# A chunked mLSTM cell and gelu block on one core: two weight sums made one chunk earlier, and one row copy set between two gelu halves

## The chip, the cores and the metric

The kernel runs on one core of one Trainium2 chip. The metric is the device time of one execution in microseconds (us), as the median over several executions. The engines are named as the profile names them: PE is TensorE (matmuls) and PEld its weight loads, DVE is VectorE, ACT is ScalarE, POOL is GpSimd, SP is SyncE, whose queue issues most of the DMAs. All of them run side by side and wait for each other by semaphores.

## What is computed

```python
def _attn_ref(q, k, v, i_gate, f_gate, o_gate):      # B, H, S, D = 4, 8, 768, 40
    for t in range(S):
        m_new = np.maximum(f_gate[:, :, t] + m, i_gate[:, :, t])
        f_stab = np.exp(f_gate[:, :, t] + m - m_new)
        i_stab = np.exp(i_gate[:, :, t] - m_new)
        C = f_stab * C + i_stab * outer(v_t, k_t)
        n = f_stab * n + i_stab * k_t
        y[:, :, t] = sigmoid(o_t) * (C @ q_t) / np.maximum(np.abs(n . q_t), 1.0)

x = y.transpose(0, 2, 1, 3).reshape(3072, 320)
h = x @ w_in                                          # w_in 320 x 2048
g = h * (1.0 / (1.0 + np.exp(-1.702 * h)))
return g @ w_out                                      # w_out 2048 x 320
```

All data are float32. The weights come as 64-bit words of which the kernel makes float32 on the core.

## The kernel before

**Chunks.** The 768 steps are cut in six chunks `w` = 0 to 5 of 128 steps (for all four batches, so 512 tokens a chunk). For each chunk the kernel has two parts that PE runs one after the other: the first product (`x @ w_in`, 16 blocks of 128 hidden columns taken as eight pairs `j`) with the gelu, and the second product (`g @ w_out`). The attention part of the next chunk (scores, values, the carried state, gates) is cut in pieces and put between the blocks of the second product: `attention(w + 1)` gives a table of pieces by block number, and the loop at L986 runs block `i` and then the pieces of that number. The schedule is manual: the order in which the program issues instructions is the order on each engine, and an instruction waits for the data and buffers it needs.

**First chunk and later chunks.** In chunk 0 the products are plain (`up`, L614, and `down`, L785, the latter 16 calls of four matmul groups, blocks 0 to 15). From chunk 1 on they are Strassen-like fast products (`up_fast`, L707, and `down_fast`, L831) of seven block products in place of eight. They need sums of the blocks of the weights. `weight_sums(n)` (L801) makes the four sums of the second weights, each one POOL subtraction of 128 x 1280 elements: n = 0 gives `t1 = w01 - w00`, n = 1 gives `t2 = w11 - t1`, n = 2 overwrites `w01` with `w11 - w01`, n = 3 gives `t4 = w10 - t2`. `w00` to `w11` are quarters of `w_out_sb`, and `t1`, `t2`, `t4` lie in `t_sb`, whose room holds keys of chunk 1 (`k_1`, read by PE for the transposes and in `carry`, L594) and a piece of raw weights before. The first product of the sums is the third block of `down_fast(1, 0)`.

**A pair in `up_fast`.** For each pair `j` PE makes products into four PSUM banks: `p1`, `p56` and two row banks `row0`, `row1`. `ps_m` is a pool of four banks taken in turn, `ps_a` one of two double banks. At j = 0 and j = 4 (`k == 0`) the row banks are fresh ones of `ps_m`, and PE then adds the products of the last 64 input columns for four pairs (`row_product`, L694, matmuls at L701), into two pairs of `ps_a` banks and, for pair j + 1, into the two banks that `p1` and `p56` had. So the `p1` of pair 5 takes the bank that `row0` of pair 4 had. For each pair ACT copies `p1` (L761), DVE makes the sums (L762, L763, L774, L775), ACT copies `row0` into `g` (`copy_row`, L739, for j < 6), and POOL adds the DVE sums to it (L781). The gelu of pair j - 1 (`gelu_fast`, L688: half 1, then half 0, both L690) is issued in pair j; half 1 needs only DVE's L775 of pair j - 1, half 0 needs POOL's L781 of pair j - 1. In pairs with `k == 2` `copy_row` is called early, before L761; in the others it is called after both gelu halves.

**POOL in chunk 1.** After pair 0, `gates(2)` runs on DVE (L288 to L326) and `wait_for(ends[2])` (L592, a copy of one column into `mark`) makes POOL wait for it. Then `weight_sums(j)` follows each of the pairs 0 to 3, and `hidden_difference` (L812, POOL) follows the pairs 2 to 5.

**Around the first chunk's scores.** `scores(1, 0)` and `scores(1, 1)` come behind block 6: PE's L459, then one DVE multiplication each (L462, into `wt[1, 0]` and `wt[1, 1]`). Behind block 8 come `values(1, 0)` and the transfers `seam_out`/`seam_in` of its half, behind block 9 `values(1, 1)` and the transfers of the other half, behind blocks 12 and 14 the two `seam_turn` (L572), which fill the `xT` that the next first product reads; behind blocks 11 and 13 the `input_sums` (L668 to L671). `values` ends in `outputs` (L464): DVE's L517 and L518, three small ones (L469, L470, L471), L473, and two L478, which write the `y` that `seam_out` sends. `token_sums` (L679 to L684) then makes the sums of `xT` for the fast product; L682 makes `x4`, the right-hand side of product 4. All of this is one queue of DVE.

Of the kernel before, what the change touches and what calls it, by code (L numbers as in the profile page):

```python
# [26 lines left out]
def kernel(  # L27
# [141 lines left out]
    wt = {(0, b): gp.tile([L, NP, 2, L], FP, tag="g", name="wt") for b in range(B)}  # L169
# [63 lines left out]
    def convert(n):  # L233
        convert_begin(n)
        convert_end(n)
# [101 lines left out]
    def banks(name):  # L337
        return ps_a.tile([128, 2, 512], FP, tag="a", name=name)
# [251 lines left out]
    def wait_for(x):  # L590

        G.tensor_copy(out=mark[0:x.shape[0]], in_=x[:, 0:1])  # L592
# [92 lines left out]
        temps[w] = {1: b11, 2: b21, 3: b22, 4: x4, 5: x1, 6: x2, 7: b12}  # L685
        second[w] = r[1][:, half_w:W]

    def gelu_fast(w, j):  # L688
        for i in (1, 0):
            A.activation(out=gs[w, j][:, i, :], in_=gs[w, j][:, i, :], func=AF.Gelu_apprx_sigmoid)  # L690

    row_banks = {}

    def row_product(w, j, start):  # L694

        n = 2 if w == NW - 2 or (w == NW - 3 and j < 2) else 1
        for h in range(n):
            t = slice(h * W // n, (h + 1) * W // n)
            for i, row in enumerate(row_banks[w, j]):
                r = slice(i * 64, i * 64 + 64)  # L700
                T.matmul(row[:, t], w_in_x[r, j, :], xT[w][r, 2].rearrange("p b t -> p (b t)")[:, t],  # L701
                         start=(start and h == 0), stop=(not start and h == n - 1))

    def bank(name="p_h"):
        return ps_m.tile([128, W], FP, tag="m", name=name)

    def up_fast(w, j):  # L707

        x = temps[w]
        k = j % 4
        left, right = slice(0, half_w), slice(half_w, W)
        f = lambda c, i: w_in_sb[:, c, (2 * j + i) * 128:(2 * j + i + 1) * 128]

        def product(n, out, start, stop):
            a = {1: lambda: f(0, 0), 2: lambda: f(1, 0), 3: lambda: s_in[:, 2, j], 4: lambda: f(1, 1),  # L720
                 5: lambda: s_in[:, 0, j], 6: lambda: s_in[:, 1, j], 7: lambda: f(0, 1)}[n]()
            T.matmul(out, a, x[n], start=start, stop=stop)  # L722

        def row_0():
            product(2, row0[:, left], k == 0, False)
            product(3, row0[:, right], False, k > 0)

        def row_1():
            product(4, row1[:, left], k == 0, False)
            product(7, row1[:, right], False, k > 0)  # L730

        y = work.tile([L, 2, DM + 64], FP, tag="y", name="parts").rearrange("p a b -> p (a b)")
        u2 = second[w]
        g = gs[w, j] = gp.tile([128, 2, W], FP, tag="g", name="g")
        apart = j < NF // 2 - 2

        def copy_row():
            if apart:
                A.copy(out=g[:, 0, :], in_=row0)  # L739

        if k == 2:
            row0, row1 = row_banks[w, j]
            row_1()
            row_0()
        p1, p56 = bank(), bank()
        if k == 0:
            row0, row1 = row_banks[w, j] = bank(), bank()
        elif k != 2:
            row0, row1 = row_banks[w, j]
        product(1, p1[:, left], True, True)  # L750
        if k == 0:
            row_0()
        product(5, p56[:, left], True, True)
        product(6, p56[:, right], True, True)
        if k != 2:
            row_1()
        if k % 2:
            row_0()
        if k == 2:
            copy_row()  # L760
        A.copy(out=y[:, left], in_=p1[:, left])  # L761
        V.tensor_tensor(out=u2, in0=p56[:, right], in1=y[:, left], op=OP.add)  # L762
        V.tensor_tensor(out=y[:, 2 * half_w:3 * half_w], in0=p56[:, left], in1=u2, op=OP.add)  # L763
        if k == 0:
            row_product(w, j, False)
            for n in (2, 3):
                both = banks("p_h")
                row_banks[w, j + n] = both[:, 0, :], both[:, 1, :]
                row_product(w, j + n, True)
            row_banks[w, j + 1] = bank(), bank()  # L770
            row_product(w, j + 1, True)
        if j:
            gelu_fast(w, j - 1)
        V.tensor_tensor(out=y[:, half_w:2 * half_w], in0=row1[:, right], in1=u2, op=OP.add)  # L774
        V.tensor_tensor(out=g[:, 1, :], in0=row1, in1=y[:, half_w:3 * half_w], op=OP.add)  # L775
        u = y.rearrange("p (a t) -> p a t", t=half_w)[:, 0:3:2]
        g0 = g[:, 0, :].rearrange("p (a t) -> p a t", a=2)
        if apart:
            if k != 2:
                copy_row()  # L780
            G.tensor_tensor(out=g0, in0=g0, in1=u, op=OP.add)  # L781
        else:
            V.tensor_tensor(out=g0, in0=row0.rearrange("p (a t) -> p a t", a=2), in1=u, op=OP.add)
# [17 lines left out]
    def weight_sums(n):  # L801
        out, a, b = ((t1, w01, w00), (t2, w11, t1), (w01, w11, w01), (t4, w10, t2))[n]
        G.tensor_tensor(out=out, in0=a, in1=b, op=OP.subtract)
# [60 lines left out]
    def run(calls):  # L864
        for f, *args in calls:
            f(*args)
# [62 lines left out]
    for w in range(NW):  # L929
        more = w + 1 < NW  # L930
        if w == 0:
            for j in range(NF // 2):
                if j % 2 == 0:
                    ahead, behind = converted[j // 2]
                    run([(convert, p) for p in ahead] + [(fetch, p) for p in fetched.get(j // 2, ())])
                    up(w, j, lambda: run([(columns_turn, 1) if p is None else (convert, p) for p in behind]))
                if j == 6:
                    load(1, "o")
                if j == 1:
                    wait_for(w_in_sb[:, 1, 512:1024])  # L940
                    scale(0, 1)
                    load(1, "v")
                if j < B and j % 2:
                    carry(0, j // 2)
                if j == 3:
                    masks()
                    gates(1)
                    columns_in(1)
                if j == 4:
                    spread(1)  # L950
                    load_squares(1, "q")
                if j >= B:
                    transposes(1, j - B)
        else:
            token_sums(w)
            for j in range(NF // 2):
                up_fast(w, j)
                if more and j == 0:
                    gates(w + 1)
                    load(w + 1, "o")  # L960
                    if w == 1:
                        wait_for(ends[w + 1])
                if w == 1 and j < 4:
                    weight_sums(j)
                if more and j == 2:
                    columns_in(w + 1)
                    spread(w + 1)
                    load(w + 1, "vk")
                if more and j:
                    for n in ((0, 2), (), (4,), (6, 1, 3), (5, 7), (), ())[j - 1]:  # L970
                        block_transposes(w + 1, n)
                if more and j == 7:
                    columns_turn(w + 1)
                if 2 <= j < 6:
                    hidden_difference(w, j - 2)
                if j >= 6:
                    hidden_sums(w, (j - 6,), G)
            gelu_fast(w, NF // 2 - 1)
            hidden_sums(w, (2, 3), V)
        side = attention(w + 1) if more else {}  # L980
        if w == 0:

            blocks = [(lambda b=b, n=n: down(w, b, n)) for n0 in (0, 2) for b in range(B) for n in (n0, n0 + 1)]
        else:
            blocks = down_fast(w, 0) + down_fast(w, 1)
        for i, block in enumerate(blocks):  # L986
            if w == 0 and i in (0, 4, 5):
                convert((17, 18, 19)[max(i - 3, 0)])
                if i == 0:
                    for n in (1, 3, 5, 7):  # L990
                        block_transposes(1, n)
            if w + 2 < NW and i == (6 if w == 0 else 0):
                load_gates(w + 2)
            if w + 2 < NW and i == 13:
                load_squares(w + 2, "kq" if w else "k")
            if w == 0 and i == 15:
                load_squares(w + 2, "q")
            block()
            run(side.get(i, []))
            if w == 0 and i in (11, 13):  # L1000
                input_sums(slice(0, 4) if i == 11 else slice(4, 8))

# [29 lines left out]
```

## Time and profile before

| what | value |
|---|---|
| median of 3 runs | 466.53 us (466.46 to 466.73) |
| span of the profiled execution | 464.1 us |
| PE busy | 456.6 us, 98% of the span, 5071 matmuls |
| PEld busy | 391.2 us, 84% |
| DVE busy | 349.2 us, 75% |
| ACT busy | 185.8 us, 40% |
| POOL busy | 162.8 us, 35%, 154 instructions |
| DMA | 52.87 MB, mean 114 GB/s |
| POOL's L803 (the weight sums) | 4 of 2.885 to 2.902 us |
| POOL's L781 | 30 of 1.256 to 1.286 us |
| ACT's L739 (`copy_row`) | 30 of 0.564 to 0.589 us |

The page gives the span of the profiled execution, not a device time of its own; the median of the runs is 2.4 us above this span. The span counts from the first to the last recorded instruction. Busy time is an average over stages: a matmul that is in flight counts as busy whether the clock is full or half. The second product of chunk 0 lies at 66 to 110 us of the span, the first product of chunk 1 at 109 to 145 us, its second product at 145 to 185 us; the first product of chunk 2 starts at 185 us.

### The profile page before, as it was taken

What the parts mean: (1) busy time and instruction counts of PE and PEld (TensorE: products, weight loads), DVE (VectorE), ACT (ScalarE), POOL (GpSimd) and SP (SyncE); (2) the same over time, 40 slices, a digit from 0 to 9 for tenths busy, and PEclk for the clock granted to TensorE, in tenths of its full rate; (3) what the DMA queues carried; (4) which work ended last, traced back from release to release, by engine and by line L of the source; (5) the groups of instructions that cost most, each with busy time, mean ns of one, the idle gap of its engine ahead of it and who ended that gap; (6) DMA issues with size and microseconds to landing.
All of it is one profiled execution on the core that took longest, in us unless ns stands there. A gap on an engine that the chain in (4) does not pass through costs nothing.

```text
span 464.1 us, 12384 instructions
## 1 busy us (share of the span) xinstructions
PE 456.6 (98%) x5071; PEld 391.2 (84%) x5071; DVE 349.2 (75%) x738; ACT 185.8 (40%) x433; POOL 162.8 (35%) x154
## 2 busy tenths in 40 slices
PE   8999999999989999999999999999999999999996
PEld 6867877776859999779999779999888999787996
DVE  6788998799958785888786888787788766553722
ACT  5686779000536700455800354900264910164200
POOL 5101508000797700266800167610157710146200
PEclk9999999999989999999999999999999999999999
DMA  8998999049976025969024978315999305000000
GB/s 169 187 295 187 253 239 204 4 106 198 149 157 78 3 59 123 200 113 189 9 58 107 194 119 162 53 33 125 175 140 156 63 18 140 29 1 1 1 28 30
DMA packets 135561, 52.87 MB, mean 114 GB/s; under 512 B 101984, under 2 KB 131632, under 8 KB 135504
## 3 DMA queue, kind: packets, MB, share of 16 engines
q1 hardware_dynamic: 127136, 50.27, 55.4%
q10 hardware_dynamic: 8048, 1.66, 1.8%
q8 instruction: 40, 0.66, 0.6%
q0 software_dynamic: 320, 0.15, 0.2%
q14 instruction: 17, 0.14, 0.1%
HBM read 44.52 MB, written 7.54 MB: 112 GB/s over the span
## 4 chain that ended last, share of the span: by engine, by line
PE 88%; SPq 4%; DMA 2%; issue 2%; DVE 2%; POOL 1%; ACT 1%; DVEq 0%; POOLq 0%; ACTq 0%
PE p_out L844 33%; PE p_h L722 24%; PE p_out L790 8%; PE p_h L701 7%; PE p_h L626 5%; SPq L122 3%; PE p_c L602 3%; PE p_o L503 2%; PE p_s L459 2%; PE p_i L511 2%; DMA s_in<-in_moe_w_in_dram 2%; PE p_h L635 2%; POOL g L781 1%; SPq L167 0%; PE p_t L386 0%
## 5 line engine op out<-in xcount | busy, mean ns | idle before, releaser
L781 POOL TENSOR_TENSOR g<-g,parts 128x512 f32<-128x512 f32 x30 | 38.2, 1272 | 196.5 <-ACT g L739 187.7
L761 ACT COPY parts<-p_h 128x256 f32<-128x256 f32 x40 | 14.9, 372 | 164.5 <-PE p_h L722 134.1
L844 PE MATMUL p_out<-w_out_sb,g 128*128 128x160 f32 x480 | 68.9, 300 | 0.0
L722 PE MATMUL p_h<-xT,w_in_sb 128*128 128x256 f32 x240 | 66.4, 385 | 2.0 <-ACT g L739 2.0
L844 PEld LDWEIGHTS p_out<-w_out_sb,g 128*128 128x128 f32 x480 | 66.4, 190 | 0.5
L690 ACT ACTIVATE g<-g 128x512 f32<-128x512 f32 x80 | 47.8, 629 | 30.1 <-DVE g L775 19.1
L722 PEld LDWEIGHTS p_h<-xT,w_in_sb 128*128 128x128 f32 x240 | 44.9, 191 | 14.2 <-issue 5.5
L849 DVE TENSOR_TENSOR o_sb<-o_sb,p_out 128x160 f32<-128x160 f32 x70 | 21.4, 317 | 44.2 <-PE p_out L844 43.6
L844 PE MATMUL p_out<-t_sb,s 128*128 128x160 f32 x320 | 47.1, 300 | 0.0
L844 PEld LDWEIGHTS p_out<-t_sb,s 128*128 128x128 f32 x320 | 44.4, 190 | 0.2
L722 PE MATMUL p_h<-t_x,s_in 128*128 128x256 f32 x160 | 42.0, 385 | 0.0
L435 ACT ACTIVATE wt<-wt,cols 128x64 f32<-128x64 f32 x160 | 38.8, 334 | 0.1
L701 PE MATMUL p_h<-xT,w_in_x 64*128 64x512 f32 (+1 forms) x200 | 37.1, 514 | 0.0
L790 PE MATMUL p_out<-w_out_sb,g 128*128 128x320 f32 x128 | 35.7, 436 | 0.0
L722 PEld LDWEIGHTS p_h<-t_x,s_in 128*128 128x128 f32 x160 | 31.0, 194 | 4.4
L762 DVE TENSOR_TENSOR t_x<-p_h,parts 128x256 f32<-128x256 f32 x40 | 16.9, 424 | 20.3 <-PE p_h L722 12.9
L790 PEld LDWEIGHTS p_out<-w_out_sb,g 128*128 128x128 f32 x128 | 23.9, 190 | 9.6
L701 PEld LDWEIGHTS p_h<-xT,w_in_x 64*128 64x128 f32 x200 | 18.5, 186 | 14.9 <-issue 13.9
L739 ACT COPY g<-p_h 128x512 f32<-128x512 f32 x30 | 17.5, 582 | 31.1 <-PE p_h L701 17.5
L626 PE MATMUL p_h<-xT,w_in_sb 128*128 128x256 f32 x128 | 29.6, 384 | 0.0
L775 DVE TENSOR_TENSOR g<-p_h,parts 128x512 f32<-128x512 f32 x40 | 27.6, 691 | 1.4
L626 PEld LDWEIGHTS p_h<-xT,w_in_sb 128*128 128x128 f32 x128 | 23.6, 190 | 5.3 <-issue 2.4
(205 smaller groups left out, 853.6 us busy)
## 6 DMA issues: line engine op xcount, KB each, us to landing
q_sq<-in_q_dram SPq DMA_DIRECT2D x20, 320.0 KB, 10.6
wt<-m_row SPq DMA_DIRECT2D x20, 256.0 KB, 5.4
k_sq<-in_k_dram SPq DMA_DIRECT2D x16, 320.0 KB, 6.0
out_dram<-o_sb SPq DMA_DIRECT2D x24, 160.0 KB, 1.9
eo<-in_o_gate_dram SPq DMA_DIRECT2D x5, 640.0 KB, 7.9
bits<-in_moe_w_in_dram SPq DMA_DIRECT2D x6, 512.0 KB, 11.3
q_sq<-x_row SPq DMA_DIRECT2D x10, 256.0 KB, 3.0
v_st<-in_v_dram SPq DMA_DIRECT2D x14, 160.0 KB, 5.7
```

The lines of the kernel that those rows point to most:

```text
L435: A.activation(out=x[:, h, :], in_=x[:, h, :], func=AF.Exp, scale=-1.0, bias=cols[w][:, c * PH + h:c * PH + h + 1])
L626: T.matmul(ph[j][i][:, t], w_in_sb[:, c, f * 128:(f + 1) * 128], x[:, c, t], start=(first and c == 0 and n == 0), stop=(not first and c == ...
L690: A.activation(out=gs[w, j][:, i, :], in_=gs[w, j][:, i, :], func=AF.Gelu_apprx_sigmoid)
L701: T.matmul(row[:, t], w_in_x[r, j, :], xT[w][r, 2].rearrange("p b t -> p (b t)")[:, t], start=(start and h == 0), stop=(not start and h == ...
L722: T.matmul(out, a, x[n], start=start, stop=stop)
L739: A.copy(out=g[:, 0, :], in_=row0)
L762: V.tensor_tensor(out=u2, in0=p56[:, right], in1=y[:, left], op=OP.add)
L775: V.tensor_tensor(out=g[:, 1, :], in0=row1, in1=y[:, half_w:3 * half_w], op=OP.add)
L781: G.tensor_tensor(out=g0, in0=g0, in1=u, op=OP.add)
L790: T.matmul(po, gs[w, f // 2][:, f % 2, b * L:(b + 1) * L], w_out_sb[:, f, :], start=(f == 0), stop=(f == NF - 1))
L844: T.matmul(po, a(f), b[:, f, :], start=(f == 0), stop=(f == NH - 1))
L849: V.tensor_tensor(out=dst, in0=x, in1=po, op=OP.add)
```

## The change

Two edits in the program, with one call site added and one loop bound altered.

1. The sums n = 0 and n = 1 are issued in chunk 0's second product, behind the pieces of block 6 (the scores of chunk 1), after a `wait_for` on one column of `wt[1, 0]`, which DVE's first L462 writes. In chunk 1's first product the sums n = 2 and n = 3 then follow the pairs 0 and 1; nothing follows the pairs 2 and 3.
2. In chunk 1's pair 4, `copy_row` is called between half 1 and half 0 of the gelu of pair 3, and no longer after it. No other pair and no other chunk is touched.

One POOL instruction (the added `wait_for`) is new; the number of all others is as before.

```diff
-    def gelu_fast(w, j):
+    def gelu_fast(w, j, between=None):
         for i in (1, 0):
+            if between and i == 0:
+                between()
             A.activation(out=gs[w, j][:, i, :], in_=gs[w, j][:, i, :], func=AF.Gelu_apprx_sigmoid)
...
+        early = w == 1 and j == 4
         if j:
-            gelu_fast(w, j - 1)
+            gelu_fast(w, j - 1, copy_row if early else None)
...
         if apart:
-            if k != 2:
+            if k != 2 and not early:
                 copy_row()
             G.tensor_tensor(out=g0, in0=g0, in1=u, op=OP.add)
...
-                if w == 1 and j < 4:
-                    weight_sums(j)
+                if w == 1 and j < 2:
+                    weight_sums(j + 2)
...
             block()
             run(side.get(i, []))
+            if w == 0 and i == 6:
+                wait_for(wt[1, 0][:, 0, 0, :])
+                weight_sums(0)
+                weight_sums(1)
```

## The prediction

> **What bounds the kernel now.** I read the chain that ended last first. From the start of chunk 0's products to the end it is PE almost throughout; the one place past 31 us where it leaves PE for long is chunk 1's first product, from 113.8 to 134.3 us, where it goes through DVE's gates, POOL's sums and ACT. Its end, with the same 42 matmuls in chunk 2 beside it (columns: start, length, what):
>
> ```profile
> 131.87 1.25 POOL g L781
> 133.11 0.02 issue
> 133.14 0.63 ACT g L690
> 133.77 0.48 ACT g L739
> 134.25 0.04 issue
> 134.29 11.02 PE p_h L722 x42
> ...
> 207.28 9.26 PE p_h L722 x42
> ```
>
> POOL's L781 (pair 3) lets ACT do half 0 of pair 3's gelu, behind which stands `copy_row` of pair 4, which frees the bank for pair 5. PE's last row product before it ends at 132.25 (L701, 128.55 + 3.70). And the 42 matmuls that follow take 11.02 us here, 9.26 in chunk 2. Second I asked for busy time and granted clock by stretches:
>
> ```profile
> 132.25:134.30 2.05, 0.01 (x2) 0.01 (x1) 1.86 (x3) 1.10 (x2) 2.05 (x2) 1.00 0.60 237
> 134.30:138.00 3.70, 3.70 (x9) 2.98 (x10) 0.81 (x2) 0.90 (x2) 3.70 (x3) 0.54 1.22 206
> ```
>
> The columns are length, PE, PEld, DVE, ACT, POOL busy, then granted clock. PE is idle for 2.04 us, POOL busy for all of it, and the clock is then 0.54 on average for 3.7 us. The loss of the place is 2.04 of idle time and 11.02 - 9.26 = 1.76 of slow matmuls, **3.80 us**. Chunks 2 to 5 have no such idle time on the chain.
>
> Third, POOL's order of time (start, length, instruction):
>
> ```profile
> 114.87 1.26 POOL L781 TENSOR_TENSOR g<-g,parts 128x512 f32<-128x512 f32 x1 [34.23 <-ACT g L739]
> ...
> 127.75 2.89 POOL L803 TENSOR_TENSOR w_out_sb<-w_out_sb 128x1280 f32<-128x1280 f32 x1
> 130.60 1.26 POOL L812 TENSOR_TENSOR g<-g 128x512 f32<-128x512 f32 x1
> 131.84 1.27 POOL L781 TENSOR_TENSOR g<-g,parts 128x512 f32<-128x512 f32 x1
> ```
>
> From 119.4 to 139.6 POOL works without a gap, four sums of 2.9 us among it, and pair 3's L781 stands behind three of them. Before it, POOL is idle from 80.6 to 114.9 us. Fourth, DVE's order of time, where the sums are to go:
>
> ```profile
> 70.27 1.45 DVE L257 TENSOR_SCALAR w_out_sb<-w_out_sb 128x512 uint32<-128x512 uint32 x1
> ...
> 87.61 2.35 DVE L462 TENSOR_TENSOR wt<-p_s,wt 128x1024 f32<-128x1024 f32 x2
> ...
> 93.87 0.17 DVE L469 TENSOR_SCALAR den<-u 128x16 f32<-128x16 f32 x1
> 94.08 0.18 DVE L470 TENSOR_TENSOR den<-u,den 128x16 f32<-128x16 f32 x1
> ...
> 100.94 0.49 DVE L794 COPY o_sb<-p_out 128x320 f32<-128x320 f32 x1 [0.44 <-PE p_out L790]
> ...
> 111.10 0.42 DVE L682 TENSOR_TENSOR t_x<-xT,t_x 128x256 f32<-128x256 f32 x1
> ```
>
> DVE has only 0.44 us of idle time between 92.1 and 112.9, the one shown before L794. Its `x4` (L682) is ready at 111.52 and PE's product 4 starts at 111.57: PE has no slack there.
>
> **Part 1, what is removed.** POOL's start stays: `mark` at 119.40, then a sum 119.54 to 122.41, L781 of pair 1 to 123.65, a sum to 126.52, L781 of pair 2 to 127.77, all as now, only that the sums are n = 2 and 3. Here the old third sum falls out. L812 for pair 0 runs 127.75 to 129.0. L781 of pair 3 needs ACT's `copy_row` of pair 3, which ends at 128.92 as now (it follows the gelu half released by L781 of pair 2): POOL runs it 129.05 to 130.3, where it now ends at 133.11. So half 0 of pair 3's gelu is released 2.8 us earlier, and even without part 2 `copy_row` of pair 4 would run behind it at about 130.85 to 131.45. That is 0.8 us ahead of 132.25, when PE asks for the bank. The whole stall and with it the half clock go: -3.80. After it: L812 of pair 1 to 131.55, L781 of pair 4 (copy and sums there by 130.25) to 132.8, L812 of pair 2 to 134.05. ACT's L761 of pair 5 comes at about 132.9 (0.67 behind the end of L701, as in chunk 2), and half 0 of pair 4's gelu at 133.8, for which L781 is there. `copy_row` of pair 5 in chunk 2 starts 3.3 us after L701 ends and is set by PE; here that is 135.5. From there the stage is chunk 2's.
>
> Does a stall come later in its place? In chunk 2 the stage runs with PE idle nowhere. The transfers are the one thing that is not tied to PE: the last `v_st` transfer lands at about 143.9 (issued by 138.35, 5.6 us) against POOL's L588 at 149.82, which moves to about 146.0; the last `k_st` at about 148.7 (issued by 143.26, 5.4 us) against PE's L602 at 154.0, which moves to 150.2. Both stay 1.5 us or more ahead: 0.
>
> **Part 1, what is added.** POOL gets `mark` and two sums behind L462. The first L462 ends at 88.82 (87.61 + 1.21). The wake-up is 0 to 0.15 us (`mark` at 119.40 behind L326's end at 119.41; L781 at 198.98 behind L763's end at 198.83), `mark` takes 0.14 from start to start, a sum 2.87 start to start and 2.90 at the last: both end at 94.73 to 94.88, say 94.8. No POOL instruction is behind them until 114.87, so POOL's queue pays nothing. PE and ACT show no wait here. SP's and POOL's DMA queues are not passed by anything: the sums issue no DMA.
>
> DVE pays. At 70.27 L257 took 1.45 us while POOL ran L588 (from 70.16), and 0.43 at 67.92 with POOL idle; the pair of L829 at 152.11 took 1.62 under L588 and L579 where one alone is 0.42, and its second ended 0.28 behind POOL's first L579. So a DVE instruction whose operands are all in SBUF waits until POOL's running instruction ends. Instructions with one operand in PSUM don't: L762 and L763 are 0.42 under L803, L849 is 0.32 under L588. L462's second half, L517 and L518 read PSUM: free. L469 (93.87) and L470 (94.08) read SBUF and start before 94.8. If L469 is held it ends at about 94.9 and L470 starts there, 0.8 late; if only L470 is held (no row shows so small a one-input instruction beside POOL) it ends at 94.9 for 94.26, 0.6 late; the lower bound, if so small ones slip through, is 0. I take 0.8, since L469 is nearest to L257, which has one input too and was held.
>
> The Trainium skill speaks against the change here: "SBUF — State Buffer", section "Who interferes with whom", says that DVE and GpSimd take a shared port pair as an exclusive lock, and that a `tensor_scalar` in a two-port mode and any instruction with two SBUF inputs block against a GpSimd read until it ends. By the page L469 and L470 are both held, the 0.8 case; by the two-input row alone it would be the 0.6 case.
>
> Behind L470 everything on DVE is back to back up to the 0.44 us of idle time before L794, which absorbs that much: **0.8 - 0.44 = 0.36 us** reaches L572, the token sums and `x4`, and PE, which has no slack there, waits as long before product 4 (or spread over products 5, 6 and 4). Bounds: 0 and, if the seam's transfers decide in place of DVE, the whole 0.8. They move by the whole 0.8, as `y` does: the second half's last `x_rest` is issued by 105.9 and lands 2.5 us behind its issue, at 107.8 to 108.4, and its first reader is the second L572 of that half at about 108.8, so they have 0.4 to 1.0 us to spare beyond which they would add to the 0.36. DVE's own delay of 0.36 adds to that room. I take nothing. What is late next is `gates(2)` and so `mark` at 119.40, by the same 0.36; PE is late by the same, so the room of 0.8 at 132.25 is untouched. An idle piece of 0.36 us is far from the 2.04 that went before the half clock; I charge no slow matmuls for it.
>
> **Part 2.** `copy_row` of pair 4 needs `row0` of pair 4 complete: the first four of the 16 row products, by about 128.55 + 0.93 = 129.5. Half 1 of pair 3's gelu ends at 129.72, so the copy runs 129.65 to 130.25, while half 0 waits for POOL's 130.3 anyhow. It costs nothing and, with part 1 in place, gives nothing: the room at PE grows from 0.8 to 2.0 us. If the row products were late, half 0 would wait up to 0.6 behind the copy; its readers (L812 of pair 3, behind 136) have time.
>
> **Sum.** 464.1 - 2.04 - 1.76 + 0.36 = 460.7 of span; with the 2.4 us that the median lies above this span, 466.53 - 3.44 = **463.1 us**.
>
> **Rivals.**
> - *No lock on the small instructions*, or absorbed: 466.53 - 3.80 = 462.7. For it: no row has a 16-column instruction beside POOL. Against: L829 and L257.
> - *The seam decides*: the whole 0.8 is paid, perhaps 0.4 more by a late `x_rest`: 463.5 to 463.9. For it: `x_rest` made L572 wait 0.2 us once. Against: the room above.
> - *A shorter stall stays* before pair 5 or 6, enough for a half clock: with, say, 0.7 of idle time left and the 1.76, 466.53 - 2.04 + 0.7 + 0.36 = 465.5; without the half clock 463.8. For it: POOL still works without a gap from 119.4 to 134. Against: 0.8 us of room without part 2, 2.0 with it.
> - *Slower*: the lock at the seam. If POOL's sums began only as DVE reaches L469, by a wait that I don't see, DVE could stand behind both: 5.8 us less 0.44 is 5.3 on PE, 1.5 over the gain; 468.0, and 469.8 with a half clock. It decides from a delay of 3.80 + 0.44 = 4.2 us on, a start of the first sum behind about 92.6. Against: its only late input, L462's first half, is done at 88.82, and `w_out_sb` and `t_sb` are free (last conversion 87.6, `carry` 76.9).
> - *The change does not do what it says*: part 2 has no effect of its own. That is my forecast for it.
>
> **How the numbers follow.** The forecast (0 < delay < 0.5, no stall) 0.64, its own range 462.8 to 463.4; no lock 0.10; the seam 0.13; a shorter stall 0.10; slower 0.03. The range 462.6 to 463.9 takes the first three and leaves out about 0.14. What can be told from no change in this kernel is 0.2%, 0.93 us: faster means below 465.6, which the first three and nine tenths of the fourth give: 0.95; within 0.2%: 0.02; slower 0.03.
>
> **What would show it.** In the profile after: two L803 at about 89 to 94.8 and two at 119.9 and 124.0 (that 0.36 later); L469 or L470 of the first `outputs` with about 1 us; no idle time before L794; a PE wait of about 0.4 near 111.5; no PE idle time before pair 5, clock 1.00 there, 42 matmuls in 9.26. I am wrong if the clock still falls near 132, if PE's wait near 111 is over 0.8 or not there, or if an idle stretch of PE comes up between 135 and 155.

## The result, and the profile after

The changed kernel takes 463.68 us (median of 13 executions) beside 466.53 for the kernel before: a ratio of 0.9925, with a 95% interval of 0.9899 to 0.9951. Two later comparisons on other occasions gave 0.9927 (0.9905 to 0.9950) and 0.9941 (0.9919 to 0.9962). All executions together have medians of 463.07 us (31 of the changed kernel) and 466.25 (73 of the kernel before): 3.2 us faster. The forecast was 463.1.

The first profile of the changed kernel fell in a disturbed execution of 469.65 us and isn't read here; the lines are from a later one of the same kernel, 463.44 us with a span of 461.7. In the changed kernel the lines of the code lie 2 or 3 further down: L701 is now L703, L722 L724, L739 L741, L761 L763, L781 L784, L794 L797, L803 L806, L812 L815, L844 L847.

First the place of the stall, in the chain of what ended last (start, length, what) and in the busy time by stretches (length, PE, PEld, DVE, ACT, POOL, granted clock):

```profile
129.27 3.63 PE p_h L703 x16
132.90 9.26 PE p_h L724 x42
142.16 8.69 PE p_out L847 x64
```

```profile
129.20:132.90 3.70, 3.70 (x18) 1.53 (x17) 3.29 (x6) 1.89 (x4) 3.70 (x4) 1.00 0.23 49
132.90:142.10 9.20, 9.20 (x44) 8.12 (x44) 8.15 (x14) 4.50 (x10) 6.54 (x7) 1.00 0.98 192
```

PE goes from the row products into pair 5 without a pause, the clock is full, and the 42 matmuls take 9.26 us as in chunk 2. The stall and its slow matmuls, 3.80 us in the profile of before, are gone. Then the place where two of the sums went, POOL and DVE in order of time:

```profile
89.17 0.19 POOL L592 COPY mark<-wt 128x1 f32<-128x1 f32 x1 [8.68 <-DVE wt L462]
89.32 2.91 POOL L806 TENSOR_TENSOR t_sb<-w_out_sb 128x1280 f32<-128x1280 f32 x1
92.31 2.89 POOL L806 TENSOR_TENSOR t_sb<-w_out_sb,t_sb 128x1280 f32<-128x1280 f32 x1
```

```profile
87.47 2.35 DVE L462 TENSOR_TENSOR wt<-p_s,wt 128x1024 f32<-128x1024 f32 x2
...
93.68 1.55 DVE L469 TENSOR_SCALAR den<-u 128x16 f32<-128x16 f32 x1
95.26 0.18 DVE L470 TENSOR_TENSOR den<-u,den 128x16 f32<-128x16 f32 x1
```

L469 takes 1.55 us in place of 0.17: it ends at 95.23, when POOL's second sum ends (92.31 + 2.89 = 95.20). The idle time that DVE had before the copy of the first product's block (L794, now L797) is gone. PE pays at pair 0:

```profile
109.17 1.03 PE L724 MATMUL p_h<-xT,w_in_sb 128*128 128x256 f32 x4
110.23 0.70 PE L724 MATMUL p_h<-xT,s_in 128*128 128x256 f32 x2
111.09 1.16 PE L724 MATMUL p_h<-t_x,s_in 128*128 128x256 f32 x4 [0.16 <-DVE t_x L679]
```

Before, these starts were 109.35, 110.22 and 110.65. Measured in the order of time from the start of the scores (L459), where both kernels are still alike, the second group of row products starts 45.95 us later here (83.25 to 129.20) and 45.11 before (83.44 to 128.55). So the moved sums cost PE some **0.83 us** in this execution (the first group of row products, at 113.28 and 112.63, gives the same). In the chain of what ended last, where these rows start 0.07 to 0.08 later, the stretch is 45.94 us here (83.33 to 129.27) and 45.92 in another execution without a late transfer (the run with the moved sums alone, 83.94 to 129.86, below).

### The profile page after: what moved, and what is told of

Its sections match the earlier page's. It is cut to its first block, busy times and chain, and to the rows that moved or that the text cites. A ratio compares the mean times of both kernels' runs of the same rounds, so it can differ in the third digit from the quotient of the medians.

```text
span 467.9 us, 12387 instructions
## 1 busy us (share of the span) xinstructions
PE 458.8 (98%) x5071; PEld 392.5 (84%) x5071; DVE 347.1 (74%) x738; ACT 186.2 (40%) x433; POOL 161.5 (35%) x155
## 4 chain that ended last, share of the span: by engine, by line
PE 77%; DMA 9%; SPq 6%; DVE 4%; ACT 2%; issue 1%; DVEq 0%
PE p_out L847 31%; PE p_h L724 25%; PE p_h L703 8%; PE p_out L793 5%; DMA bits<-in_moe_w_out_dram 3%; SPq L122 3%; DMA bits<-in_moe_w_in_dram 3%; PE p_o L503 2%; PE p_s L459 2%; PE p_i L511 2%; DMA q_sq<-in_q_dram 2%; SPq L167 2%; PE p_c L602 1%; SPq L120 1%; ACT wt L435 1%
## 5 line engine op out<-in xcount | busy, mean ns | idle before, releaser
L784 POOL TENSOR_TENSOR g<-g,parts 128x512 f32<-128x512 f32 x30 | 38.2, 1273 | 186.3 <-ACT g L741 174.8
L763 ACT COPY parts<-p_h 128x256 f32<-128x256 f32 x40 | 14.9, 372 | 167.2 <-PE p_h L724 162.1
L847 PE MATMUL p_out<-w_out_sb,g 128*128 128x160 f32 x480 | 68.9, 300 | 0.0
L847 PEld LDWEIGHTS p_out<-w_out_sb,g 128*128 128x128 f32 x480 | 66.4, 190 | 0.5
L724 PE MATMUL p_h<-xT,w_in_sb 128*128 128x256 f32 x240 | 65.9, 383 | 0.0
L724 PEld LDWEIGHTS p_h<-xT,w_in_sb 128*128 128x128 f32 x240 | 44.6, 190 | 11.9 <-issue 6.3
L847 PE MATMUL p_out<-t_sb,s 128*128 128x160 f32 x320 | 47.1, 300 | 0.0
L847 PEld LDWEIGHTS p_out<-t_sb,s 128*128 128x128 f32 x320 | 44.4, 190 | 0.2
L724 PE MATMUL p_h<-t_x,s_in 128*128 128x256 f32 x160 | 41.1, 379 | 0.0
L435 ACT ACTIVATE wt<-wt,cols 128x64 f32<-128x64 f32 x160 | 38.8, 333 | 0.1
L793 PE MATMUL p_out<-w_out_sb,g 128*128 128x320 f32 x128 | 37.7, 453 | 0.0
L703 PE MATMUL p_h<-xT,w_in_x 64*128 64x512 f32 (+1 forms) x200 | 37.1, 514 | 0.0
L724 PEld LDWEIGHTS p_h<-t_x,s_in 128*128 128x128 f32 x160 | 30.4, 190 | 4.2
L793 PEld LDWEIGHTS p_out<-w_out_sb,g 128*128 128x128 f32 x128 | 25.1, 199 | 10.4 <-issue 1.4
L703 PEld LDWEIGHTS p_h<-xT,w_in_x 64*128 64x128 f32 x200 | 18.5, 186 | 14.9 <-issue 14.2
L741 ACT COPY g<-p_h 128x512 f32<-128x512 f32 x30 | 17.5, 582 | 32.4 <-PE p_h L703 17.9
```

The source lines that it names most:

```text
L435: A.activation(out=x[:, h, :], in_=x[:, h, :], func=AF.Exp, scale=-1.0, bias=cols[w][:, c * PH + h:c * PH + h + 1])
L793: T.matmul(po, gs[w, f // 2][:, f % 2, b * L:(b + 1) * L], w_out_sb[:, f, :], start=(f == 0), stop=(f == NF - 1))
L847: T.matmul(po, a(f), b[:, f, :], start=(f == 0), stop=(f == NH - 1))
```

## The experiments

**The changed kernel once more.** No edit.

> The changed kernel once more, for a profile without a late transfer before block 6. My theory (the stall before pair 5 and its half clock gone for 3.80 us, DVE's small instructions held by POOL's second sum for 0.36 us on PE): no PE idle time at pair 5, clock 1.00 there, the 42 matmuls in 9.26 us; L469 or L470 of the first outputs ends at about 94.9, 0.6 to 0.8 us late, and PE waits some 0.4 us near 111.5; 463.1 us. Rival (the small instructions slip through beside POOL): L469 and L470 take 0.17 and 0.18 us and start at 93.9 and 94.1, no wait of PE; 462.7 us.

Median 462.94 us of 12. No stall at pair 5, 9.26 us for the 42 matmuls. L469 was held in this execution too and took 2.39 us: its transfers came late, so the conversions, L462 and the sums were 1.7 us late, and the second sum ended only at 97.03. So the cost of the lock (DVE standing still until POOL's running instruction ends) varies with how late L462 is against the first values. That some 0.4 us would be paid was too low; that nothing is held is refuted.

**Only the moved sums.**

```diff
-        early = w == 1 and j == 4
+        early = False
```

> Only the moved sums; the row copy of pair 4 stands behind both gelu halves again. My theory: the copy ends at about 131.5 (plus what DVE's delay adds), still 0.8 us ahead of the end of the row products, so PE does not stop: the time of the whole change, 463.1 us, within 0.2. Rival (the early copy is what frees the bank in time): a stall of some tenths to 2 us stays before pair 5, with or without the half clock; 464 to 466 us.

Median 462.66 us of 6 (ratio 0.9916, 0.9888 to 0.9944). No idle time of PE at pair 5: the late row copy ends at 132.25 (131.68 + 0.57), and the row products end at 133.50. Part 2 is not needed once the sums are out of the way; the room is 1.2 us without it.

**Only the early row copy.**

```diff
-            if w == 0 and i == 6:
-                wait_for(wt[1, 0][:, 0, 0, :])
-                weight_sums(0)
-                weight_sums(1)
...
-                if w == 1 and j < 2:
-                    weight_sums(j + 2)
+                if w == 1 and j < 4:
+                    weight_sums(j)
```

> Only the early row copy; all four sums in chunk 1's first product as before. My theory: the copy ends at about 130.3 and PE goes straight on at 132.25, but POOL is as late as before: L781 of pair 4 ends at about 138.4, half 0 of pair 4's gelu and behind it the row copy of pair 5 end at about 139.6, and PE asks for that bank at about 137.0 for pair 6: 2.6 us of idle time there, probably with the half clock; no gain, 466.5 us, within 0.8. Rival (the copy alone cures the stall): no idle time of PE in the stage, 462.7 us.

Median 464.70 us of 12 (ratio 0.9967, 0.9948 to 0.9985): between the two. PE and ACT in order of time, in this kernel:

```profile
137.38 0.59 PE L724 MATMUL p_h<-xT,w_in_sb 128*128 128x256 f32 x2
137.81 1.03 PE L724 MATMUL p_h<-t_x,s_in 128*128 128x256 f32 x4
140.04 0.70 PE L724 MATMUL p_h<-xT,w_in_sb 128*128 128x256 f32 x2 [1.20 <-ACT g L741]
```

```profile
138.88 0.63 ACT L692 ACTIVATE g<-g 128x512 f32<-128x512 f32 x1 [3.93 <-POOL g L784]
139.42 0.57 ACT L741 COPY g<-p_h 128x512 f32<-128x512 f32 x1
```

The stall moved as the theory had it, from the row copy of pair 4 to the row copy of pair 5, behind the gelu half that POOL releases. Its place and size were wrong. Seven products, 14 matmuls, make a pair; the first of the last 14 is the one that waits, so it is `p1` of pair 7, and `p1` of pair 6, which the theory let wait from 137.0, runs at 137.38 without a wait. PE asks at 138.8, so it waits 1.20 us for 2.6, and the clock stayed at 1.00 (mean 0.999 or more in all 12 executions). POOL is still late behind it, and in chunk 1's second product PE waits again, which it does in neither the kernel before nor the changed one. The waits of that stretch in the run with the early copy:

```profile
PE p_s L459 <- DVE state L611: 0.8, 2, 0.5
```

So 2.3 us won in the first product (14.4 from the row products to the end of the 42 matmuls for 16.8) becomes 1.5 at the end: 0.8 is given back at the scores of chunk 2, whose inputs come from ACT and DVE. On DVE's side the lock is seen again. DVE's own last sums (L823 and L826 here, L820 and L823 before) take 3.10 and 3.47 us for 1.35 and 1.29: in the kernel before, POOL's last sum ends at 147.65 as DVE's begin (147.63), and its L588 starts only at 149.82, whereas here POOL works on beside them, from 145.12 to 151.48. Whether ACT's part would bound the scores without this was not tried.

**The kernel before with PE kept busy in its stall.**

```diff
     mark = const.tile([L, 1], FP, name="mark")
+    zeros = const.tile([128, 256], FP, name="zeros")
+    G.memset(zeros, 0.0)
...
             row_banks[w, j + 1] = bank(), bank()
             row_product(w, j + 1, True)
+            if w == 1 and j == 4:
+                for _ in range(4):
+                    T.matmul(row_banks[w, j + 2][0][:, 0:256], zeros[:, 0:128], zeros, start=False, stop=False)
```

> The kernel before, with four matmuls of a zero tile (128 x 256 each, some 0.44 us apiece) added into a row bank of pair 6 behind the row products of pair 4, so that PE is busy for about 1.8 of the 2.04 us in which it waits. My theory (the half clock comes from the idle time): PE goes on with pair 5 at 134.3 as before, at clock 1.00, the 42 matmuls take 9.26 in place of 11.02 us; 466.53 - 1.76 = 464.8 us. Rival (the 42 matmuls are slow for another reason, such as the transfers or POOL's work in that stretch): 11.0 us again, 466.5 us.

Median 465.39 us of 12 (ratio 0.9976, 0.9955 to 0.9997). Order of time of PE here (L776 are the added matmuls, L724 pair 5):

```profile
132.08 1.99 PE L776 MATMUL p_h<-zeros 128*128 128x256 f32 x8
133.91 0.64 PE L724 MATMUL p_h<-xT,w_in_sb 128*128 128x256 f32 x2
134.39 1.03 PE L724 MATMUL p_h<-t_x,s_in 128*128 128x256 f32 x4
```

And the busy time of the stretch of pairs 5 to 7 (length, PE, PEld, DVE, ACT, POOL, clock):

```profile
134.07:143.05 8.98, 8.98 (x44) 7.89 (x43) 6.55 (x12) 4.54 (x10) 8.90 (x7) 1.00 1.02 178
```

With the idle time filled the clock is 1.00 and the matmuls behind it have their usual lengths: the slow ones came from the idle time, not from the transfers or POOL. Eleven of the 12 executions have a mean clock of 0.998 or more, one 0.995; no trace shows where that one lost it. The whole gain of 1.76 doesn't arrive: PE waits 0.7 us at L461 (the scores, in this kernel's numbering) for DVE's state, as in the run before, and the kernel before loses the 1.76 only in some of its executions, as comes next.

**How often the half clock comes.** Of the 60 executions of the kernel before whose clock is on record, 34 have a mean granted clock of 0.996 or less, the other 26 one of 0.998 or more. One stretch of 3.4 us at half clock in 464 us makes 0.996, so I take the 34 for executions with the half clock at the stall; only one such execution was profiled. The medians are 466.57 and 465.72 us. So the half clock is not there in every execution, and where it is absent only 0.85 of its 1.76 us arrives, probably for the reason just seen (none of these 26 was profiled). Of the changed kernel's 31 executions one has such a clock, the one of 469.65 us, and its profile shows it between 87 and 95 us, behind an idle time of PE of 2.38 us at the scores, not at the old stall. The Trainium skill, "TensorE: Matmul & The Clock Gate", section "Part 1: The HAM clock gate (the "warmup" mystery)", says that the gate looks at a free-running window of about 3.4 us; the slow stretch in the profile of before is 3.4 us long (clock 0.50 from 134.60 to 138.00), and a free-running window would fit with a stall that sets it off in only a part of the executions, though no run here shows where the window began. The page's idle window of about 3.4 us before the clock falls is longer than the 2.04 us seen here, and the measurement decides.

**A third sum behind the scores.** The sum n = 1 is made twice with the same values.

```diff
                 weight_sums(0)
                 weight_sums(1)
+                weight_sums(1)
```

> The changed kernel with the sum n = 1 made a second time right behind itself (same values, so the output stays). My theory (DVE's small instructions of the first outputs wait for POOL's running sum, and what is over 0.44 us of it reaches PE): POOL works some 2.9 us longer, to about 98.7; one of L469, L470, L471 takes 2.5 us or more on top of the 1.3 us of the changed kernel; PE waits about 3.5 us in all before product 3 or 5 of pair 0: 462.9 + 2.9 = 465.8 us, to 467.5 with a half clock behind that wait. Rival (PE's delay there comes from late transfers, not from POOL): POOL idle until 115 anyway, so 462.9 us.

Median 466.81 us of 12 (ratio 1.0010, 0.9983 to 1.0036): the whole gain is lost to one more POOL instruction on an engine that is idle until 115 us. DVE, POOL and PE in order of time:

```profile
94.15 1.74 DVE L469 TENSOR_SCALAR den<-u 128x16 f32<-128x16 f32 x1
95.92 0.18 DVE L470 TENSOR_TENSOR den<-u,den 128x16 f32<-128x16 f32 x1
96.14 0.25 DVE L471 RECIPROCAL den<-den 128x16 f32<-128x16 f32 x1
96.31 3.24 DVE L473 SCALAR_TENSOR_TENSOR eo<-eo,u 128x640 f32<-128x640 f32 x1
```

```profile
95.94 2.93 POOL L806 TENSOR_TENSOR t_sb<-w_out_sb,t_sb 128x1280 f32<-128x1280 f32 x1
```

```profile
113.33 0.70 PE L724 MATMUL p_h<-xT,s_in 128*128 128x256 f32 x2 [2.67 <-DVE xT L572]
114.20 2.07 PE L724 MATMUL p_h<-t_x,s_in 128*128 128x256 f32 x4 [0.17 <-DVE t_x L679]
```

L469 waits for the second sum, L473 (0.76 alone) for the third, and PE stands 2.67 us at product 3 of pair 0. In this profile the half clock follows (the 2.07 for 1.16 is its trace); the four executions with a clock of 0.999 or more have a median of 464.69, the eight with 0.996 or less 467.5. That is the slower rival of the prediction, seen at work: it only needed POOL's sums to reach 2.9 us further into the outputs.

**The two sums apart.** Sum 0 behind the scores, sum 1 behind the token sums of chunk 1, where DVE's next instructions read PSUM.

```diff
                 weight_sums(0)
-                weight_sums(1)
...
             token_sums(w)
+            if w == 1:
+                wait_for(xT[1][64:128, 2].rearrange("p b t -> p (b t)"))
+                weight_sums(1)
```

> The sum n = 0 behind the first chunk's scores, the sum n = 1 between token_sums and pair 0 behind a wait for the last token sum (L684), the rest as in the changed kernel. My theory: the first sum ends at about 92.3, ahead of L469, so nothing is held there, and L469 takes 0.17 us; the second runs from about 112.6 to 115.5, beside DVE instructions that read PSUM, and delays L288 and L784 of pair 0 by some 0.6 us, for which there is room; the 0.8 us of the lock come back: 462.9 - 0.8 = 462.1 us. Rival 1 (the held L469 costs PE nothing): 462.9. Rival 2 (L288 held behind a whole sum delays the gates and with them the pairs): 463.5 or more.

Median 462.57 us of 6 (ratio 0.9917, 0.9901 to 0.9934). The median lies between the theory's 462.1 and the first rival's 462.9, and the trace decides: L469 takes 0.17 us and PE follows the times of before up to the stall, without the stall. DVE, POOL and the chain of what ended last:

```profile
93.86 0.17 DVE L469 TENSOR_SCALAR den<-u 128x16 f32<-128x16 f32 x1
```

```profile
112.34 2.90 POOL L806 TENSOR_TENSOR t_sb<-w_out_sb,t_sb 128x1280 f32<-128x1280 f32 x1
```

```profile
128.60 3.63 PE p_h L703 x16
132.24 9.26 PE p_h L724 x42
```

The second sum and POOL's L784 hold L288 (0.63 us) and L290 (1.17 for 0.28), but `mark` for the gates starts at 119.40 as before. The profile's span is 460.3, 3.8 below that of the kernel before.

**One sum moved.** Sum 0 behind the scores, sums 1 to 3 behind pairs 0 to 2, early copy kept.

```diff
                 weight_sums(0)
-                weight_sums(1)
...
-                if w == 1 and j < 2:
-                    weight_sums(j + 2)
+                if w == 1 and j < 3:
+                    weight_sums(j + 1)
```

> Only the sum n = 0 behind the scores; n = 1 to 3 follow pairs 0 to 2; early row copy kept. My theory: no lock at L469 (the sum ends at about 92.3); L784 of pair 3 is as late as in the kernel before (to about 133.1), but the early copy frees pair 5's bank at 130.3 and L784 of pair 4 ends at about 135.6, so the row copy of pair 5 ends at 136.8, ahead of PE's request at about 138.5: no idle time of PE, and POOL's later work is 0.8 us later than in the changed kernel, which may just do: 462.1 us, up to 462.9 where the later POOL work holds the scores of chunk 2 as in the run with the early copy alone. Rival (both sums must go, or PE stops before pair 5 or 6): an idle time of 1 us or more, 463.5 to 465.

Median 463.03 us of 6 (ratio 0.9935, 0.9916 to 0.9954). Nothing is held at L469 (0.18) and PE has no idle time in the first product, with 9.26 us for the 42 matmuls, so the rival is out. But 0.7 us of PE's time is missing between 152 and 160 us (7.28 busy of 8.00), where the chain runs through ACT's L435 and DVE's state:

```profile
154.33 1.46 DVE state L579
```

The later work is felt by way of the lock. POOL's last sum ends 15.59 us behind the start of the second row products (128.61 to 144.20; 15.32 in the changed kernel, 129.20 to 144.52), and this L579, which takes 0.50 us in the changed kernel, starts 0.04 behind POOL's L439 (154.29) and takes 1.45. In the changed kernel it starts 0.07 ahead of it (154.81 and 154.88). About a tenth of a microsecond decides there; this is read from the two traces, and no run tests it.

**Without the added wait.** The sums start as soon as POOL is free.

```diff
             if w == 0 and i == 6:
-                wait_for(wt[1, 0][:, 0, 0, :])
                 weight_sums(0)
```

> The changed kernel without the added wait: the sum n = 0 starts as soon as POOL is free, at about 80.7 us, n = 1 when the last piece of the second weights is there (about 87.6). My theory (a DVE instruction with its operands in SBUF waits for POOL's sum): the additions to the state and the conversions at 80.7 to 84 are held, up to 2.9 us; L462 and with it the first values come up to 1.5 us late, since L462's first half ends 1.1 us ahead of the matmuls that need it; but the second sum then ends at about 90.6, ahead of L469: between 462.1 and 463.9 us. Rival (no lock): 462.1 us, with all DVE instructions at their usual lengths.

Median 463.77 us of 9 (ratio 0.9950, 0.9928 to 0.9972), with a spread of 462.59 to 466.29; the slowest two have a mean clock of 0.996, and no trace shows where they lost it. The lock now hits a conversion:

```profile
82.49 2.60 DVE L256 TENSOR_SCALAR w_out_sb<-w_out_sb 128x512 f32<-128x512 f32 x1
```

That is 0.42 us alone, held by POOL's sum from 81.65 to 84.80. L469 is free in turn (0.17). The time is not told apart from the changed kernel's.

**The changed kernel and the split one side by side.** No new edit.

> The changed kernel beside the split version on one chip. My theory (0.8 us of the lock reach PE in an undisturbed execution): 462.9 us, and the split version 0.4 to 1.0 us below it; L469 of the first outputs takes 1.3 to 2.4 us. Rival (the 0.8 us are lost in what varies at the start of an execution): the two medians within 0.2 us.

> The split version again. My theory: 462.3 us, 0.4 to 1.0 below the changed kernel of the same call, no DVE instruction held at the first outputs, no half clock in any execution. Rival: 462.9 us, within 0.2 of the changed kernel.

462.97 and 462.59 us, 6 executions each; with the earlier ones 463.07 (31) and 462.59 (12). In the traces of these two runs the split version gains 0.84 us between the scores and the second row products (45.10 for 45.94). In the medians it is 0.4 to 0.5 us, which the spread of single executions (nearly all from 461.85 to 466.72 and all from 461.72 to 463.88) does not make certain. The split version is the best found, and beats the kernel before clearly; that it beats the changed kernel is shown in the trace only.

## Why the prediction was right, step by step

- **The stall and its slow matmuls, 3.80 us: right.** They are gone in every profile with both sums moved, and the filled stall shows that 1.76 of it was the clock. What the step didn't know is that the slow part comes in a part of the executions (by the mean clock 34 of 60); between those with and without it lie 0.85 us and not 1.76.
- **L784 of pair 3 earlier by 2.8 us, POOL's order behind it: right.** From the start of `mark` behind the gates it comes after 9.59 us here (119.65 to 129.24) and after 12.44 before (119.40 to 131.84), 2.85 earlier. `mark` itself is only 0.44 late against the scores where PE is 0.83 late, so the room of the row copy without part 2 is 1.2 us and not the 0.8 that was to stay as it is. `copy_row` of pair 5 starts 3.26 us behind the end of L703 (136.16 against 132.90); 3.3 was forecast.
- **Part 2 worth nothing beside part 1: right**, as the moved sums alone show. But the last rival's sentence that it has no effect of its own was wrong: alone it is worth 1.5 us, since it shrinks the idle time to 1.20 us and with it removes the half clock.
- **DVE held at L469 and nothing else on POOL's way: right in mechanism, too small in size.** The term was 0.8 us at L469 and 0.36 on PE. It measured 1.38 (1.55 for 0.17) and some 0.83, above the 0.8 that the prediction had named as a sign of being wrong there. That is the size of the seam rival's 0.8, but not its cause: L572 waited for no transfer. That L469 is held, which has one input, bears out the case of 0.8 against that of 0.6. The size failed in two rows that I took for the start of the sums. The wake-up was put at 0 to 0.15 us; `mark` starts 0.49 us behind the end of L462's first half (87.47 + 1.21 = 88.68 to 89.17). And from sum to sum I took 2.87 us, the distance to an L781 that doesn't need the sum; the second sum reads the first one's result and starts 2.99 behind it. (In the kernel before, POOL's L823, which reads the result of L820, also starts 1.35 behind it, 142.44 to 143.79, where one that doesn't starts 1.23 behind, 143.79 to 145.02.) Together 0.5 late; why the wake-up is 0.49 here and 0.13 behind L684 in the split version (111.95 to 112.08) was not tried.
- **0.44 us of DVE's idle time absorbs that much, the rest reaches PE one for one: right to 0.1 us.** 1.38 - 0.44 = 0.94 against 0.83 measured.
- **The seam's transfers add nothing: right** in the executions without a late transfer (no DMA wait before L572).
- **2.4 us between span and time: wrong.** Every execution with both numbers shows 1.7 to 1.8 (463.44 for a span of 461.7, 464.80 for 463.1). So the profiled execution of before was one of about 465.8 us, below the median of 466.53 that I set against it. The forecast was made as a difference, of 3.44 us; it is 3.80 - 0.83 = 3.0 by the traces and 3.2 by the medians of all executions. That 463.1 agrees to 0.1 us with the median of all 31 executions is in part luck: the start of the sum was 0.3 too high (466.53 in three executions, 466.25 in 73) and the cost of the lock 0.5 too low, and the two nearly cancel.

## What to carry to other kernels

An engine that is idle is not free: before work is moved into POOL's idle time, look at what DVE runs beside it, and choose a stretch where DVE reads PSUM; the same two sums of 2.9 us cost nothing set apart beside readers of PSUM, 0.8 us behind the scores, and a third one there cost all of the gain. Where one engine's lateness shows as a stall of another, moving one releaser (the early copy) takes the stall to the next buffer, and what is left of the lateness is paid at the next place where it is needed. And a stall of 2 us can cost nearly 2 more by the clock behind it, but not in every execution: compare mean clocks before a difference of half a per cent is explained.

## What the runs showed of the hardware

- An instruction as small as L469 (16 columns, 0.17 us) waits for the whole rest of a POOL instruction, 1.3 to 2.2 us here; but RECIPROCAL (L471) ran in its usual 0.25 us at 96.14, inside POOL's third sum (95.94 to 98.87), and L470 got in between two sums that stood back to back.
- The profiled idle time of PE, and how many executions of that kernel have a mean clock of 0.996 or less: 2.04 us, 34 of 60; 2.67 + 0.17 us, 8 of 12 (the third sum); 1.20 us, none of 12 (the early copy alone). With the 2.04 us filled by matmuls of zeros it is 1 of 12.
